# A fused attention and MoE kernel: one list of steps for all engines, named PSUM banks, and two more batches transposed by DMA

## The chip, the cores and the metric

The kernel runs on one core of one Trainium2 chip. The metric is the device time of the kernel in microseconds; lower is better. Three runs of the kernel before took 324.28, 325.44 and 326.56 us, so the median is 325.44 us.

## What is computed

Sliding-window attention with a distance bias (a query sees itself and the 127 keys before it), and behind it a feed-forward layer whose activation is a Swish with its own beta for each hidden unit. The attention output, heads side by side, is the layer's input.

```python
B, H, S, D = q.shape                      # 8, 8, 576, 64
scores = (1.0 / np.sqrt(D)) * np.matmul(q, k.transpose(0, 1, 3, 2))
rel = pos[:, None] - pos[None, :]
mask = (rel >= 0) & (rel < 128)
scores = np.where(mask, scores - slopes[:, None, None] * np.abs(rel), -1e9)
attn = softmax(scores)
x = np.matmul(attn, v).transpose(0, 2, 1, 3).reshape(B * S, H * D)   # 4608 x 512
h = x @ w_in                              # 512 x 2048
g = h * (1.0 / (1.0 + np.exp(-beta * h)))
out = g @ w_out                           # 2048 x 512
```

## The kernel before

The 4608 tokens are worked on in two tilings at once. Attention goes by batch (8 batches of 576 tokens, each in four query blocks of 128 and a tail of 64). The feed-forward layer goes by group (9 groups of 512 tokens). Batches and groups don't line up: group g needs tokens 512g to 512g+511, so group 2 needs blocks 0 to 2 of batch 2, group 3 the last two blocks of batch 2 and blocks 0 to 2 of batch 3, and so on.

For batch b of 2 to 7 the steps are these:

- q and k arrive in f32 by DMA issued from SP (`get`, L207; the buffers are `fst`, 14 of them), GpSimd casts them to bf16 (`cast_qk`, L228 and L229, buffers `bst`, 4 of them), and SP issues a transposing DMA into `qkT` (`DT`, L413). v comes by a casting DMA of GpSimd (`get_v`, L250).
- S: `SC` (L438) multiplies keys by queries for a pair of heads; each of its matmuls uses 64 rows of the array. ScalarE takes the exponential of 1024 columns (L446, about 1.02 us), and VectorE multiplies it by the decay and mask (`factor`, L171 and L176, 0.79 and 0.71 us).
- V: `PVB` (L492, L495) multiplies the weights by v for all eight heads of a block; VectorE divides by the sum (L499, L500), which gives the block's attention output `xn`.
- X: `xn` has tokens on partitions and must be transposed into `XT`, a ring of three groups. For batches 0 to 3 this is done by TensorE (L520 for batches 2 and 3: matmuls against the identity into PSUM, and a copy by ScalarE, L523). From batch `XDMA = 4` on it is a transposing DMA from SP (L512).

Batches 0 and 1 have a form of their own for the four full blocks: loads and casts by pairs of heads (`get_pair`, L218; `cast_pair`, L235), transposition on TensorE (`TP`, L287), two score visits A and B for each pair (`SP_`), `PVP`, and `XP` for the transposition of the result.

For group g, H is one of 16 hidden tiles: four matmuls of 128x512 (`Hm`, L557), a tanh on ScalarE (L564, about 0.69 us) and a product on VectorE (L565, 0.68 us) into `gT`. O is a quarter of the second product for a block of 128 tokens: four matmuls of 128x512 (`OS`, L588); after four of them ScalarE copies 128x512 out of PSUM into `osb` (L598, 0.60 us; five buffers) and a DMA stores it, issued from GpSimd for groups 0 to 2, from ScalarE later, from SP for the last two (L606). The last block is done in two halves of 256 columns that share a bank; the second half's copy is VectorE's (L596). The weights W1 and W2 come by four casting DMAs each on GpSimd's queue.

The order is written by hand. The opening (batches 0 and 1, and group 0) is a list of calls. From then on `spread` lays the steps of the attention, weighted, between the H and O of the groups. PSUM banks come from pools that are opened and closed on the way (`psum_t`, `psum_x`, `psum_o`, `psum_s`). TensorE, SP and GpSimd keep the written order in the opening and later; ScalarE and VectorE keep it in the opening alone, and in the rest the scheduler may choose:

```python
    with tc.manual_schedule(engines={ENG.PE, ENG.SP, ENG.Pool}):
        with tc.manual_schedule(engines={ENG.Activation, ENG.DVE}):
            for w in ("p0", "p1", "v0", "p2", "v1", "p3", "v2", "v3"):
```

Of the kernel before, what the change touches and what calls it, by code (L numbers as in the profile page):

```python
# [15 lines left out]
P = 128  # L16


@with_exitstack
def kernel(  # L20
# [63 lines left out]
    psum_c = ctx.enter_context(tc.tile_pool(name="psum_c", bufs=1, space=bass.MemoryType.PSUM))  # L84
    psum_h = ctx.enter_context(tc.tile_pool(name="psum_h", bufs=2, space=bass.MemoryType.PSUM))
    trans = ExitStack()
    psum_t = trans.enter_context(tc.tile_pool(side="right", name="psum_t", bufs=2, space=bass.MemoryType.PSUM))
    SS = psum_c.tile([P, 2, 512], F32, name="SS")
    psum_c.seal()
    opening = ExitStack()  # L90
    psum_x = opening.enter_context(tc.tile_pool(name="psum_x", bufs=1, space=bass.MemoryType.PSUM))
    SX = psum_x.tile([P, 2, 512], F32, name="SX")
    late, gates = {"tick": 0}, {}
    spans = [SS]

    def span():

        spans.append(spans.pop(0))
        return spans[-1]

    def obank(name, tag=None):
        if tag is None:
            late["n"] = late.get("n", 0) + 1
            tag = "ops" if late["n"] % 2 else "h3"
        return late["o"].tile([P, DM], F32, name=name, tag=tag)[:]

    def after(ins, other):
        tc.add_manual_dep(
            ins.ins, other.ins.name,
            mybir.DependencyInfo(mybir.DependencyClass.Sync, mybir.DependencyReason.DATA),  # L110
            reason="gate",
        )

    def idle(n):
        for _ in range(n):
            nc.tensor.matmul(
                SS[:, 0, :], lhsT=zeros[:, 0:P], rhs=zeros[:], start=True, stop=True,
                skip_group_check=True)  # L120

    def constants():
# [4 lines left out]
        idle(8)  # L127
# [35 lines left out]
    def falls_late(i):  # L163
        to, a, w = ((0, 0, P), (128, 0, 64), (192, 0, P), (320, 1, 64), (384, 1, P))[i]
        after(nc.vector.tensor_copy(
            out=falls[:, :, to : to + w], in_=fall[:, :, a, 0:w]), gates[1, 4])

    def factor(pt, m, p):

        if m:  # L170
            nc.vector.tensor_tensor(  # L171
                out=pt[:], in0=pt[:], in1=falls[:, 2 * p : 2 * p + 2], op=ALU.mult)
            return
# [16 lines left out]
    def betas():  # L190
        bps = psum_t.tile([P, NFF], F32, name="bps", tag="t")
        nc.tensor.transpose(out=bps[:], in_=bflat[:], identity=identf[:])
        nc.vector.tensor_scalar_mul(beta_h[:], bps[:], 0.5)
# [7 lines left out]
    def get(what, b, sb):  # L201
# [5 lines left out]
        return nc.sync.dma_start(  # L207
# [4 lines left out]
    def get_pair(b, p):  # L212

        r = []
        for what, src in (("k", k), ("q", q)):
            f = fst_pool.tile([P, 2, 4, D], F32, name="fst", tag="fst")
            fs[what, b, "p", p] = f
            r.append(nc.sync.dma_start(  # L218
                out=f[:].rearrange("r h c d -> r h (c d)"),
                in_=src[b, 2 * p : 2 * p + 2, 0:FULL, :].rearrange("h (r c) d -> r h (c d)", c=4),  # L220
            ))
        return r[0]

    def cast_qk(b, sb):
        rows = ROWS[sb]
        t = bst_pool.tile([P, 2, H, D], BF16, name="bst", tag="bst")
        staged[b, sb] = t
        nc.gpsimd.tensor_copy(out=t[0:rows, 0], in_=fs.pop(("q", b, sb))[0:rows])  # L228
        return nc.gpsimd.tensor_copy(out=t[0:rows, 1], in_=fs.pop(("k", b, sb))[0:rows])  # L229

    def cast_pair(b, p):
        t = bst_pool.tile([P, 2, 4, 2 * D], BF16, name="bst", tag="bst")
        staged[b, "p", p] = t
        for i, what in ((1, "k"), (0, "q")):
            r = nc.gpsimd.tensor_copy(  # L235
                out=t[:, i].rearrange("r c (h d) -> r h c d", d=D),
                in_=fs.pop((what, b, "p", p))[:])
        return r

    def cast_v(b, sb):  # L240
        moved.add(("v", b, sb))
        rows = ROWS[sb]
        return nc.gpsimd.tensor_copy(  # L243
            out=VS[b % 2][0:rows, sb, :, 0:D], in_=fs.pop(("v", b, sb))[0:rows])
# [22 lines left out]
    pts, xns = {}, {}  # L267

    def calm(n):

        z = psum_h.tile([P, 512], F32, name="z", tag="hps")
        for _ in range(n):
            nc.tensor.matmul(
                z[:], lhsT=zeros[:, 0:P], rhs=zeros[:], start=True, stop=True,
                skip_group_check=True)

    def TP(b, p):
        src = staged.pop((b, "p", p))
        for i in (1, 0):
            if (b, p) == (0, 1):  # L280
                calm(1 + i)
            tps = psum_t.tile([P, FULL], BF16, name="tps", tag="t")
            to = tps[:].rearrange("d (c r) -> d c r", c=4)
            if i == 0:
                to = tps[:].rearrange("d (k c r) -> d c k r", k=4, c=4)
# [256 lines left out]
    def Hm(g, j, cs):  # L542
# [18 lines left out]
        if cs[-1] < NDM - 1:  # L561
            return
# [332 lines left out]
```

The softmax here doesn't subtract the row's maximum and nothing guards it: scores larger than these inputs give would overflow.

## Time and profile before

| What | Value |
|---|---|
| runs, median (lowest to highest) | 325.44 us (324.28 to 326.56) |
| span of the profiled execution, first to last instruction | 324.0 us |
| median of the runs less that span | 1.4 us |
| mean granted clock of TensorE | 0.999 of full |
| HBM read and written | 36.71 MB, 9.44 MB |
| L588, O: 592 matmuls | 28.6% of the chain that ended last |
| L557, H: 576 matmuls | 31.1% of the chain that ended last |

The profiled execution's own time isn't listed apart from its span; what lies around the span is taken from the median of the runs, 1.4 us. The chain of waits, followed back from the last instruction, is PE for 69% and DMA for 17%. Busy times of matmuls overlap: one of 128x512 is listed with 379 ns, but four that follow each other begin 0.86 us before the next four.

### The profile page before, as it was taken

Reading aid. Unit: us, or ns where it says so; the run is one execution under the profiler, and the core shown is the slowest. Engines: PE = TensorE matmul, PEld = TensorE weight load, DVE = VectorE, ACT = ScalarE, POOL = GpSimd, SP = SyncE. Lnnn points to the kernel's source line nnn. Section 1 sums busy time; section 2 is a strip of 40 time slices with the busy share of each in tenths; the row PEclk is TensorE's granted clock in tenths of the full one; section 3 lists DMA queues with packets and bytes.
Section 4 is the critical chain, followed back from the end, with each engine's and each line's share of the span. In section 5 each row is a group of like instructions: output and inputs, shape, how many; then the busy total and the mean of one; then the engine's idle time right before and its main releaser. Section 6 shows DMA issues by size and latency. Waiting matters only on the chain.

```text
span 324.0 us, 5988 instructions
## 1 busy us (share of the span) xinstructions
PE 312.7 (97%) x2297; PEld 153.3 (47%) x2297; DVE 183.1 (57%) x346; ACT 194.1 (60%) x283; POOL 98.8 (30%) x154
## 2 busy tenths in 40 slices
PE   8888999999999999999999999999999999999995
PEld 3454554443545454544454545444544455444443
DVE  5777877542548753785178717752775176335500
ACT  6857887635558865685467635845675465346511
POOL 4864820333873455356226232340000000000000
PEclk9999999999999999999999999999999999999999
DMA  7999999998999999999969994993222112110021
GB/s 221 252 263 238 176 196 196 215 199 162 214 181 208 222 208 139 230 217 148 257 153 196 150 245 94 211 138 107 18 65 60 65 18 65 46 62 32 10 90 65
DMA packets 147565, 48.84 MB, mean 151 GB/s; under 512 B 135360, under 2 KB 143824, under 8 KB 147536
## 3 DMA queue, kind: packets, MB, share of 16 engines
q1 hardware_dynamic: 115712, 32.39, 56.1%
q0 software_dynamic: 28624, 10.29, 26.1%
q10 hardware_dynamic: 3200, 5.78, 5.1%
q8 instruction: 18, 0.29, 0.4%
q14 instruction: 11, 0.09, 0.1%
HBM read 36.71 MB, written 9.44 MB: 142 GB/s over the span
## 4 chain that ended last, share of the span: by engine, by line
PE 69%; DMA 17%; SPq 6%; POOL 2%; ACT 2%; DVE 2%; issue 1%; POOLq 0%; DVEq 0%
PE ops L588 21%; PE hps L557 21%; PE hpo L557 10%; PE oph L588 7%; DMA fst<-in_v_dram 6%; DMA qkT<-bst 6%; SPq L207 3%; DMA fst<-in_q_dram 3%; DMA fst<-in_k_dram 2%; PE SS L438 2%; SPq L218 2%; PE ST L438 1%; PE SS L495 1%; PE SS L492 1%; POOL bst L229 1%
## 5 line engine op out<-in xcount | busy, mean ns | idle before, releaser
L588 PE MATMUL ops<-W,gT 128*128 128x512 bf16 (+1 forms) x464 | 109.7, 372 | 0.5 <-ACT osb L598 0.5
L565 DVE SCALAR_TENSOR_TENSOR gT<-sig,hps 128x512 bf16<-128x512 bf16 x100 | 67.6, 683 | 71.8 <-ACT sig L564 71.5
L557 PE MATMUL hps<-XT,W 128*128 128x512 bf16 x400 | 99.9, 379 | 0.3 <-DVE XT L533 0.3
L564 ACT ACTIVATE sig<-hps,beta_h 128x512 bf16<-128x512 f32 x100 | 68.1, 690 | 34.6 <-PE hps L557 33.2
L588 PEld LDWEIGHTS <-gT 128*128 128x128 bf16 x592 | 55.7, 98 | 61.6 <-issue 1.9
L557 PEld LDWEIGHTS <-W 128*128 128x128 bf16 x576 | 52.9, 98 | 60.8 <-issue 3.6
L228 POOL CAST bst<-fst 128x512 bf16<-128x512 f32 (+1 forms) x32 | 20.8, 650 | 74.4 <-DMA fst<-in_q_dram 42.4
L557 PE MATMUL hpo<-XT,W 128*128 128x512 bf16 x168 | 43.1, 379 | 0.0
L564 ACT ACTIVATE sig<-hpo,beta_h 128x512 bf16<-128x512 f32 x42 | 29.0, 690 | 16.9 <-PE hpo L557 16.9
L565 DVE SCALAR_TENSOR_TENSOR gT<-sig,hpo 128x512 bf16<-128x512 bf16 x42 | 28.6, 681 | 11.2 <-ACT sig L564 11.0
L598 ACT ACTIVATE osb<-ops 128x512 f32<-128x512 f32 (+1 forms) x28 | 16.6, 595 | 25.5 <-PE ops L588 25.5
L446 ACT ACTIVATE pt<-SS 128x1024 bf16<-128x1024 f32 x24 | 24.5, 1020 | 11.6 <-PE SS L438 11.1
L588 PE MATMUL oph<-W,gT 128*128 128x512 bf16 x128 | 29.3, 379 | 0.0
L229 POOL CAST bst<-fst 128x512 bf16<-128x512 f32 (+1 forms) x32 | 22.1, 690 | 15.6 <-DMA fst<-in_k_dram 15.0
L176 DVE TENSOR_TENSOR pt<-pt,fall 128x1024 bf16<-128x1024 bf16 x24 | 17.1, 712 | 14.8 <-ACT pt L446 14.8
L446 ACT ACTIVATE pt<-ST 128x1024 bf16<-128x1024 f32 x24 | 24.5, 1022 | 0.0
L171 DVE TENSOR_TENSOR pt<-pt,falls 128x1024 bf16<-128x1024 bf16 x24 | 18.8, 791 | 9.3 <-ACT pt L446 9.3
L250 POOL DMA_DIRECT2D vs<-in_v_dram x25 | 21.3, 869 | 0.2 <-issue 0.2
L598 ACT ACTIVATE osb<-oph 128x512 f32<-128x512 f32 x8 | 4.8, 597 | 21.1 <-PE oph L588 21.1
L495 PEld LDWEIGHTS <-pt 128*128 128x128 bf16 x240 | 14.8, 97 | 4.2
L243 POOL CAST vs<-fst 128x512 bf16<-128x512 f32 (+1 forms) x15 | 10.5, 703 | 15.9 <-DMA fst<-in_v_dram 15.9
L438 PEld LDWEIGHTS <-qkT 64*128 64x128 bf16 x240 | 8.9, 94 | 12.5 <-issue 12.0
(102 smaller groups left out, 257.8 us busy)
## 6 DMA issues: line engine op xcount, KB each, us to landing
fst<-in_k_dram SPq DMA_DIRECT2D x32, 256.0 KB, 6.0
fst<-in_q_dram SPq DMA_DIRECT2D x32, 256.0 KB, 5.3
out_dram<-osb ACTq DMA_DIRECT2D x22, 256.0 KB, 2.0
fst<-in_v_dram SPq DMA_DIRECT2D x12, 256.0 KB, 5.4
out_dram<-osb POOLq DMA_DIRECT2D x12, 256.0 KB, 5.2
vs<-in_v_dram POOLq DMA_DIRECT2D x20, 128.0 KB, 6.1
W<-in_moe_w_in_dram POOLq DMA_DIRECT2D x4, 512.0 KB, 7.9
W<-in_moe_w_out_dram POOLq DMA_DIRECT2D x4, 512.0 KB, 12.8
```

Of the source, the lines that this page charges most:

```text
L171: nc.vector.tensor_tensor(out=pt[:], in0=pt[:], in1=falls[:, 2 * p : 2 * p + 2], op=ALU.mult)
L228: nc.gpsimd.tensor_copy(out=t[0:rows, 0], in_=fs.pop(("q", b, sb))[0:rows])
L229: return nc.gpsimd.tensor_copy(out=t[0:rows, 1], in_=fs.pop(("k", b, sb))[0:rows])
L250: return nc.gpsimd.dma_start(out=VS[b % 2][0:rows, sb, :, 0:D], in_=v[b, :, P * sb : P * sb + rows, :].rearrange("h p d -> p h d"))
L438: nc.tensor.matmul(o, lhsT=qk[64 * e : 64 * e + 64, 1, p, P * kb : P * kb + P], rhs=qk[64 * e : 64 * e + 64, 0, p, P * kb : P * kb + nq], ...
L446: nc.scalar.activation(out=pt[:], in_=sps[:], func=ACTF.Exp, scale=qscale)
L495: nc.tensor.matmul(o, lhsT=weights(b, qb, h, 0), rhs=vs[:, qb, h, 0 : D + 1], start=qb == 0, stop=True, skip_group_check=True)
L557: nc.tensor.matmul(hps, lhsT=W1[:, c, bass.ts(j, P)], rhs=XT[:, c, c0 : c0 + TOKG], start=(c == 0), stop=(c == NDM - 1),)
L564: gates[g, j] = nc.scalar.activation(out=sig[:], in_=hps, func=ACTF.Tanh, scale=beta_h[:, j : j + 1])
L565: gates["gT"] = nc.vector.scalar_tensor_tensor(out=gts[g][:, j, :], in0=sig[:], scalar=1.0, in1=hps, op0=ALU.add, op1=ALU.mult)
L588: nc.tensor.matmul(ops_[:, cols], lhsT=gT[:, j, i * P : i * P + P], rhs=W2[:, j, cols], start=(j == 0), stop=(j == NFF - 1),)
L598: nc.scalar.mul(o, ops_[:, cols], 0.5)
```

## The change

All that the hand-written order, `spread` and the pools did is replaced by one list, `PLAN`, of some 1300 steps. A step has a name, the batch or group, the tile and, where it writes PSUM, a bank. One loop walks the list, and each engine keeps the list's order, ScalarE and VectorE too, from the first instruction to the last. PSUM is one tile of eight banks. What was one helper (matmul, then the copy or the exponential) becomes two steps, so that the second can stand elsewhere in the list.

The names: `k q` (loads of pairs), `gq gk gv` (loads of blocks), `ck cq cQ cK cv` (casts), `w1 w2`, `pv` (v by casting DMA), `D` (transposing DMA of q and k), `Rk Rq rk rq` (transposition on TensorE and copy), `A B EA EB VA VB nA nB XP xc` (batches 0 and 1), `S E M V n XD` (batches 2 to 7), `H a d` (hidden tile, tanh, product), `O oc st` (second product, copy, store), `OL lc ls` (halves of the last block), `z` (idle matmuls).

`XD`, the transposing DMA, now serves batches 2 to 7; the matmul form `X` is left for the tails of batches 0 and 1. The halves of the last block have a bank each, and the second half goes first.

```diff
-    psum_c = ctx.enter_context(tc.tile_pool(name="psum_c", bufs=1, space=bass.MemoryType.PSUM))
-    psum_h = ctx.enter_context(tc.tile_pool(name="psum_h", bufs=2, space=bass.MemoryType.PSUM))
...
+    psum = ctx.enter_context(tc.tile_pool(name="psum", bufs=1, space=bass.MemoryType.PSUM))
+    PS = psum.tile([P, 8, 512], F32, name="PS")
+    def bank(k):
+        return PS[:, k, :]
...
     def X(b, qb):
...
-        if b >= XDMA:
-            tok0 = (b * S + P * qb) % XTR
...
-        if b >= 2:
-            xt = span()[:, 0, :].rearrange("p (c q) -> p c q", c=NDM)
...
+    def XD(b, qb):
+        xnv = xns.pop((b, qb))[:].rearrange("p h d -> p (h d)")
+        for r0, r1, at in pieces(b, qb):
+            nc.sync.dma_start(out=XT[:, :, at : at + r1 - r0], in_=xnv[r0:r1], transpose=True)
...
+    with tc.manual_schedule(engines={ENG.PE, ENG.SP, ENG.Pool, ENG.Activation, ENG.DVE}):
+        for step in PLAN.split():
+            name, *at = step.split(":")
+            name, _, eng = name.partition(".")
+            STEPS[name](*([ENGINES[eng]] if eng else []), *map(int, at))
```

Parts of the list, in its order: the start; the loads and casts of the opening; the steps around the start of groups 2, 3, 4 and 5; the end.

```
const q.s:0:0 k.s:0:0 ck.p:0:0 k.s:0:1 q.s:0:1 z:2:5 order ones Rk:0:0:5 cq.p:0:0 ck.p:0:1 rk.v:0:0
cq.p:0:1 z:1:7 Rq:0:0:0 k.s:0:2 ck.p:0:2 rq.a:0:0 A:0:0:4:1 EA:0:0 k.s:0:3 q.s:0:2 Rk:0:1:1
B:0:0:6:0 z:1:4 q.s:0:3 EB:0:0 cq.p:0:2 ck.p:0:3 Rq:0:1:4 gv.s:0:1 gv.s:0:0 cq.p:0:3 z:2:6 rk.v:0:1
fr:6 fr:0 rq.a:0:1 beta:1 Rq:0:2:4 Rk:0:2:5 cv.p:0:1 gv.s:0:3 q.s:1:1 rk.v:0:2 gv.s:0:2 cv.p:0:0
q.s:1:0 k.s:1:0 rq.a:0:2 B:0:1:6:0 w1:0 fr:4 A:0:1:1:1 cv.p:0:3 EB:0:1 Rk:0:3:5 Rq:0:3:0 EA:0:1
...
cQ.p:3:0 n:2:0 M:2:1:1 M:2:1:0 M:2:1:3 gk.s:3:2 XD:2:1 gq.s:3:4 st.p:0:1 M:2:1:2 V:2:2:5 gv.s:2:3
O:1:1:0:7 O:1:0:3:2 O:1:2:2:0 O:1:1:1:7 D:3:0 XD:2:0 cQ.p:3:1 cQ.p:3:4 cK.p:3:2 st.p:0:0 cK.p:3:4
cv.p:2:3 n:2:2 O:1:1:2:7 XD:2:2 V:2:4:5 O:1:2:3:0 gq.s:3:3 H:2:0:1 a:2:0 oc.a:1:0 n:2:4 H:2:1:3
...
O:2:1:0:3 O:2:1:1:3 V:3:0:5 O:2:0:2:7 D:4:1 V:3:2:0 O:2:2:0:4 O:2:2:1:4 O:2:2:2:4 n:3:0 n:3:2
S:4:0:0:0 S:4:0:1:5 E:4:0:1 M:4:0:1 cQ.p:4:3 cK.p:4:3 st.p:1:0 cK.p:4:4 cQ.p:5:0 gq.s:4:4 XD:3:1
O:2:2:3:4 XD:3:0 XD:2:3 st.p:1:3 XD:3:2 O:2:0:3:7 cQ.p:4:4 gk.s:6:3 D:4:3 V:3:3:5 gk.s:5:4 D:4:4
gk.s:5:1 O:2:1:2:3 E:4:0:0 V:3:4:0 n:3:3 n:3:4 oc.a:2:0 H:3:1:7 O:2:1:3:3 a:3:1 H:3:0:0 H:3:4:2
...
O:2:3:3:2 pv:5:4 pv:4:2 cK.p:5:1 pv:4:3 cK.p:5:2 V:4:1:0 H:3:15:7 H:3:6:5 n:4:1 H:3:14:0 H:3:13:1
a:3:10 a:3:6 d:3:6 H:3:9:6 a:3:15 a:3:14 H:3:12:5 XD:4:1 d:3:14 oc.a:2:3 a:3:13 a:3:12 d:3:15 d:3:10
O:3:1:0:2 M:4:1:1 d:3:13 H:4:1:0 a:4:1 D:5:0 D:5:2 D:5:1 H:4:5:4 d:3:12 a:3:9 cQ.p:5:4 a:4:5 a:3:11
...
E:5:1:2 O:3:3:3:4 V:5:1:6 O:4:0:0:5 st.p:1:2 H:4:11:0 O:4:0:1:5 cK.p:6:2 d:4:12 H:4:13:3 oc.a:3:3
gq.s:6:2 a:4:11 M:5:1:2 n:5:1 H:4:14:4 O:4:1:0:1 st.a:3:0 a:4:13 O:4:1:1:1 st.a:3:2 D:6:0 M:5:1:0
d:4:9 pv:5:3 cQ.p:6:4 cQ.p:6:1 pv:5:2 a:4:14 XD:4:2 XD:5:0 cQ.p:6:2 XD:5:1 D:6:1 d:4:13 gk.s:6:4
H:5:3:7 H:5:2:6 d:4:14 d:4:11 H:5:6:4 D:6:2 gq.s:7:3 H:5:1:3 a:5:3 H:5:0:2 a:5:1 d:5:3 a:5:2 a:5:6
...
st.a:7:2 O:8:1:2:0 oc.a:8:0 lc.v:1 st.a:8:0 O:8:1:3:0 oc.a:8:1 st.a:8:1 st.s:8:2 ls.s:1 OL:0:1
lc.a:0 ls.s:0
```

## The prediction

> **What bounds the kernel now.** I read the page's first lines, then busy time by stages, then TensorE's groups by shape, then single waits in the timeline.
>
> ```profile
> span 324.0 us, 5988 instructions
> PE 312.7 (97%) x2297; PEld 153.3 (47%) x2297; DVE 183.1 (57%) x346; ACT 194.1 (60%) x283; POOL 98.8 (30%) x154
> ```
>
> TensorE is busy for 97% of the span; no other engine is above 60%. A new order can only win back PE's idle 11.3 us, or take work off PE. The stages (columns: stretch, length, then busy us and count of PE, weight loads, DVE, ACT, POOL; clock, DMA share, GB/s) tell where that idle time is:
>
> ```profile
> 0.00:8.00 8.00, 6.62 (x34) 3.09 (x34) 4.72 (x25) 5.34 (x12) 3.57 (x13) 1.00 0.75 220
> 8.00:16.00 8.00, 6.65 (x84) 3.24 (x82) 6.19 (x14) 6.50 (x9) 6.95 (x10) 1.00 1.22 251
> 16.00:24.00 8.00, 7.09 (x83) 4.07 (x84) 5.64 (x17) 4.65 (x8) 5.34 (x10) 1.00 1.19 266
> 24.00:32.00 8.00, 6.98 (x57) 3.19 (x57) 6.03 (x11) 6.35 (x11) 3.31 (x5) 1.00 1.01 241
> 40.00:48.00 8.00, 7.40 (x106) 4.50 (x101) 5.71 (x15) 6.57 (x11) 2.01 (x4) 1.00 1.23 195
> 64.00:310.00 246.00, 244.19 (x1712) 118.21 (x1711) 136.17 (x230) 145.23 (x207) 68.08 (x98) 1.00 0.86 137
> 310.00:324.00 14.00, 10.07 (x62) 5.86 (x60) 0.42 (x1) 1.73 (x4) 0.00 (x0) 0.99 0.21 76
> ```
>
> The first 48 us lose 5.3 us (1.2 of them before the first matmul), the 246 us of the steady stage 1.8, the end 3.9, of which some 3.4 is the last store after the last matmul. So the steady stage is packed already; a large gain isn't there to be had. The groups that lost something outside the opening:
>
> ```profile
> L438 PE MATMUL SS<-qkT 64*128 64x256 bf16 x72 | 8.5, 276 | 1.3 <-DMA qkT<-bst 1.3
> L520 PE MATMUL ST<-ident,xn 128*128 128x128 bf16 x16 | 1.6, 220 | 0.5 <-DVE xn L500 0.5
> L588 PE MATMUL ops<-W,gT 128*128 128x256 bf16 x32 | 3.8, 273 | 0.5 <-ACT osb L598 0.5
> ```
>
> **What the change takes off PE.** X for batches 2 and 3 was matmuls against the identity (L520): 8 blocks of four 128x128 and 2 of four 64x64. One of them in the timeline (start, length, engine, line):
>
> ```profile
> 91.00 1.02 PE L588 MATMUL ops<-W,gT 128*128 128x512 bf16 x4
> 92.27 0.40 PE L520 MATMUL ST<-ident,xn 128*128 128x128 bf16 x4 [0.24 <-DVE xn L500]
> 92.50 1.89 PE L588 MATMUL ops<-W,gT 128*128 128x512 bf16 x8
> ```
>
> The block occupies PE from 92.27 to 92.50, 0.23 us; four 128x512 take 0.86 elsewhere, so L520 could have begun at 91.86 and lost 0.40 (the 0.24 shown hides a drain of 0.17). Eight blocks of 0.23 and two of about 0.1 (64x64 follow at 25 ns) are 2.0 us; two waits of 0.40 (the other at 122.91) are 0.8. **-2.8.** The Trainium skill, "TensorE: Matmul & The Clock Gate", Back-to-back issue gap, gives some 56 ns for 128 columns isolated and about 81 with a weight load each; this trace's four in 0.23 are 58 each, and I go by those. The 10 ACT copies out of PSUM (L523, 0.6 us each) go too: 5.6 us on an engine that idles 40%, hidden under PE; no gain.
>
> **What it adds.** Ten more DMA transposes on SP's queue, for which the nearest row is the 21 that batches 4 to 7 have already:
>
> ```profile
> L512 SPq DMA_TRANSPOSE XT<-xn x21: 1171/1194/2271, 146.8 to 276.6; - x21
> DMA to landing us min/median/max: 2.3/2.8/6.5
> ```
>
> Each holds SP for 1.2 us. After 216 us, when only stores share the DMA engines, landing is 2.3 to 3.9; the twelve from 146 to 215 average 4.6. The skill's "DMA: Bandwidth & Descriptors", section Issuing engines are not separate DMA queues, says that all DMAs share the same 16 engines and interleave whoever issues them; the two halves agree, and as the new ten fall about where L520 stood, 88 to 138 us (DMA share 1.2 to 1.4), I use the loaded figures.
>
> Whether PE sees this depends on how much PE work the new list leaves between the product V of the last needed block and the first H of the group that reads it. Counting 0.86 for each four 128x512, 0.46 for a V, 0.22 for an S plus 0.24 to switch in and out of 64-row matmuls:
> - group 2: after V(2,2) six O and one V, 5.6 us;
> - group 3: after V(3,2) six O, two S, two V, 6.8;
> - group 4: after V(4,1) seven H or O, 6.1;
> - group 5: after V(5,1) seven, 6.1;
> - group 6: after V(6,0) seven O, three S, one V, 7.4; groups 7 and 8 over 9.
>
> In the kernel before, V ends at 181.7, 212.1, 245.4 and 274.8, and groups 5 to 8 begin at 191.2, 222.5, 255.0 and 285.2: 9.5 to 10.4 us, and none waits. The new list is tighter. The chain costs 1.2 us for V's end to xn's end (121.67 to 122.85), then SP, then landing L. With SP free and L=4 it is 5.2: no wait. With one more transpose ahead on SP (1.2) and L=4.6 it is 7.0: 1.4+0.2+0.9+0.9 over groups 2 to 5, 3.4. I take **+2.0**, bounds 0 and 12 (L=6.5, one ahead: 8.9, so 3.3+2.1+2.8+2.8+1.5=12.5). What is queued behind such a transpose on SP: q and k loads and the transposes D of the next batch, with S behind them.
>
> **What it moves.**
> - The score waits (L438, three of 0.43 mean idle plus 0.17, 1.8 us): q and k casts, D and loads are in a new order. Loads for batch 2 come far ahead, but D(3,1), D(3,2), D(4,1) and D(7,2) still stand right before the S that needs them, and D (L413) lands 3.1 to 7.8 us after its issue. I count half as gone: **-0.9**, bounds -1.8 and +2.
> - The last O half gets a bank of its own, and DVE's half goes first. The halves of 16 matmuls begin at 316.26 and 318.64; 16 at 109 ns are 1.74. **-0.6.** If bank 1 were late it would cost that 0.6.
> - Opening. q and k of batch 0 go ahead of v on SP; in the trace loads land about 1 us apart (the eighth at 10.9, the tenth at 12.5), so the last q/k comes at 10.9 in place of 12.5. Against that, the last v is 13th in place of 12th, after 16 us, W1's first part is issued on POOL behind two v casts (about 13.2, not 10.5), and W1's third goes behind k(1,2)'s cast, which frees the DMA for q and k of batch 1: the 1.1 us of L287's waits at 30.8. ACT's row of exponentials (8 of 0.8 to 1.0) and DVE's norms (0.6 each) end where they did, about 17.4 and 20. Of 4.1 us removable idle I take **-1.5**, bounds -4 and +3 (W1 late for H(0,4)).
> - W2's parts, the tail casts and v loads on POOL are far from their readers: O of group 0 begins after 44 us of PE work and W2 is asked for after 25 to 33. Output stores of groups 0 to 2 go later on POOL; (0,3)'s stands near the end of the v loads, so one of five osb buffers is held. ACT may then wait at the copies of group 2, each freed by a store that lands 5.2 us after issue; PE has about 3 us of other banks there. Zero; if that cover is gone, up to 3.
> - Banks by name and no pools: in the steady stage the list leaves 1.4 us or more (median 5) from an H to the next use of its bank, where tanh and product take 0.69 and 0.68. Zero; cover is PE's other banks. E, factor, V: V(2,2) follows its last S by 1.7 us, with 1.02 and 0.79 between: 0.2 inside the range. Everything else (exp, tanh, norms, idle matmuls, matmul counts, number of S groups: 25 for 24) is the same.
>
> **Sum.** -2.8 +2.0 -0.9 -0.6 -1.5 = -3.8: span 320.2. The median of the runs, 325.44, is 1.4 over the span of the profiled execution; so 321.6.
>
> **Rivals.**
> - *All waits go.* Idle that a new order can remove: 4.1 in the opening, 2.1 from 48 to 310, 0.6 at the end, 2.0 of X, and about 0.17 more per wait for some 20 of them, 3: 11.8. Span 312.2, time 313.6. For it: ACT and DVE are never above 84% in any stage. Against it: the opening runs at 240 to 266 GB/s, so data, not order, sets part of it.
> - *The gain is given back.* Each transposition leaves PE but returns as a wait before H. With L=4.6 and one ahead (3.4) and nothing won in the opening or at S: -2.8-0.6+3.4 = 0: time 325.4.
> - *Slower: SP's row becomes the path.* SP issues in order. In groups 2 to 6 the last XT transpose has loads, a D or other transposes ahead of it, and the next loads behind. At L=6.5 the waits before H are 12.5; with the other terms -5.8 that is +6.7: 332. It decides from L of about 5.6 (8.0 per chain: 2.4+1.2+1.9+1.9+0.6 = 8.0, and S waits doubled, +1.8): then +4. For it: 6.5, 6.2 and 6.4 occur in the trace; against it: the issue order there is denser in loads than the new one, which fetches k ahead.
> - *It doesn't do what it says*: the built order holds 40 matmuls and 10 copies fewer and 10 transposes more, so that is out.
>
> **Chances.** Forecast case (319 to 324) 0.45; all waits gone 0.15; given back 0.22; slower 0.18. A change under 1% (322.2 to 328.7) is about what can't be told from none here. Faster takes the second case and most of the first: 0.50; same 0.32; slower 0.18. The range leaves out the upper part of the slow case and the tip of the floor: 314 to 328.5.
>
> **What would show it.** Right: no L520-like matmul for xn, the wait between the last halves gone, small waits (under 1.5 us each) of H on DMA XT at the starts of groups 2 to 5, PE's first 48 us a little denser. Wrong on the good side: XT transposes landing in under 4 us and no H waiting. Wrong on the bad side: H or S waiting on DMA by 2 us and more each, SP's waits for xn in front of loads, or ACT held by osb with PE behind it.

## The result and the profile after

| | median | range | runs |
|---|---|---|---|
| before | 325.46 us | 324.20 to 326.56 | 20 |
| after | 327.22 us | 324.24 to 329.76 | 20 |

The ratio is 1.0043, 95% interval 1.0022 to 1.0063: the change makes the kernel slower by some 0.4% (1.8 us between the medians), where 1.2% faster was forecast, and the range of the runs is more than twice as wide. Medians and ranges, here and below, are of all runs; a ratio leaves out the runs that are over 1.5% above the fastest of their kernel, two of the new kernel's twenty, and its profiled execution is one of these two. The span of that execution is 327.6 us, that of the median run 325.4; what is said of the new list below therefore also rests on profiles of other kernels that share the list where it matters.

The first lines of the page after:

```profile
span 327.6 us, 5873 instructions
PE 311.3 (95%) x2257; PEld 152.0 (46%) x2257; DVE 183.0 (56%) x346; ACT 184.8 (56%) x273; POOL 96.0 (29%) x154
```

The 40 matmuls and 10 copies are gone, PE has less to do, and it idles 16.3 us where it idled 11.3. Busy time by stages (columns as before: stretch, length, PE, weight loads, DVE, ACT, POOL, then clock, DMA share, GB/s):

```profile
8.00:16.00 8.00, 6.73 (x76) 3.23 (x72) 5.94 (x13) 6.54 (x10) 5.05 (x8) 1.00 1.09 254
16.00:24.00 8.00, 5.50 (x87) 3.84 (x87) 6.45 (x19) 3.63 (x6) 4.02 (x6) 0.95 1.14 258
24.00:32.00 8.00, 8.00 (x49) 3.58 (x48) 3.24 (x6) 5.69 (x10) 3.02 (x5) 0.84 1.24 197
...
40.00:48.00 8.00, 6.74 (x102) 3.96 (x100) 6.50 (x18) 5.22 (x8) 6.13 (x11) 1.00 1.19 193
...
64.00:310.00 246.00, 240.83 (x1664) 115.47 (x1663) 139.46 (x235) 136.87 (x196) 66.40 (x99) 1.00 0.92 143
310.00:327.60 17.60, 13.58 (x79) 7.53 (x77) 0.42 (x1) 2.66 (x5) 0.00 (x0) 0.98 0.25 90
```

Two things are to be seen. The opening and the 246 us after it are both less dense than before (the latter loses 5.2 us, not 1.8). And the clock column isn't 1.00 from 16 to 32 us: a row with PE "8.00 busy" there hides slow work. The waits themselves, in the timeline of PE (start, length, line, tiles; in brackets the idle time and what ended it):

```profile
23.30 5.21 PE L633 MATMUL PS<-XT,W 128*128 128x512 bf16 x16 [1.71 <-DMA W<-in_moe_w_in_dram]
36.00 1.04 PE L633 MATMUL PS<-XT,W 128*128 128x512 bf16 x4 [0.32 <-DMA W<-in_moe_w_in_dram]
...
45.77 1.90 PE L633 MATMUL PS<-XT,W 128*128 128x512 bf16 x8 [1.26 <-DVE xnp L439]
71.06 1.89 PE L656 MATMUL PS<-W,gT 128*128 128x512 bf16 x8 [0.36 <-DMA W<-in_moe_w_out_dram]
74.54 0.61 PE L523 MATMUL PS<-qkT 64*128 64x256 bf16 x8 [0.49 <-DMA qkT<-bst]
90.50 0.20 PE L578 MATMUL PS<-vs,pt 128*128 128x65 bf16 x1 [0.93 <-DVE pt L262]
97.26 1.90 PE L633 MATMUL PS<-XT,W 128*128 128x512 bf16 x8 [0.71 <-DMA XT<-xn]
...
191.19 4.04 PE L633 MATMUL PS<-XT,W 128*128 128x512 bf16 x18 [1.04 <-DMA XT<-xn]
```

The first row needs reading twice: 16 matmuls take 5.21 us, where eight take 1.90 in the row at 45.77 and 16 would take 3.6. TensorE ran at half clock for 3.4 us (23.1 to 26.6 in the clock record) right behind its wait for W1, and that costs 1.7 us more than the wait. The wait at 45.77 is put down to DVE, but W1's fourth part lands at 45.72, so it is that one. Loads of W1 and W2, of before and of after (operation, count, min/median/max duration in ns, first and last issue):

```profile
L258 POOL DMA_DIRECT2D W<-in_moe_w_in_dram x4: 740/744/899, 10.5 to 32.7; - x4
L262 POOL DMA_DIRECT2D W<-in_moe_w_out_dram x4: 740/744/747, 35.1 to 39.4; - x4
```

```profile
L351 POOL DMA_DIRECT2D W<-in_moe_w_in_dram x4: 742/745/897, 13.8 to 37.8; - x4
L355 POOL DMA_DIRECT2D W<-in_moe_w_out_dram x4: 742/742/812, 40.9 to 64.3; - x4
```

The last part of W2 is issued 25 us later than before, and lands at 71.02, when its reader waits. Why, GpSimd's timeline after shows:

```profile
46.08 0.78 POOL L206 CAST bst<-fst 64x512 bf16<-64x512 f32 x1
59.64 0.61 POOL L206 CAST bst<-fst 128x512 bf16<-128x512 f32 x1 [12.78 <-DMA fst<-in_k_dram]
60.20 0.84 POOL L206 CAST vs<-fst 128x512 bf16<-128x512 f32 x1
60.98 0.81 POOL L355 DMA_DIRECT2D W<-in_moe_w_out_dram  x1
```

GpSimd stood 12.8 us at a cast of batch 2's k, whose load was issued late on SP, with two W2 loads behind it in its queue.

**One measure for all kernels below.** From the starts of PE's matmuls I sum up what each took beyond its pace in an undisturbed row (216 ns for 128x512, 109 for 128x256, 55 for 128x128, 29 for 128x65, 56 for 64 rows x 256): waits, switches and half clock together, "lost PE time", up to a time t. A wait counted so is 0.17 us longer than the idle time in brackets, as in the prediction. Idle matmuls that an experiment adds count as lost.

| lost up to | 24 us | 48 | 76 | 130 | 250 | 316 |
|---|---|---|---|---|---|---|
| before | 9.3 | 14.1 | 15.9 | 20.0 | 23.9 | 24.3 |
| after | 11.0 | 16.5 | 18.5 | 22.9 | 29.4 | 29.8 |
| after's list, last bank alone changed (d_lastbank) | 11.2 | 14.8 | 19.6 | 23.3 | 28.6 | 28.8 |

The work itself sums to 295.4 us before and 293.5 after. The last two rows are of one and the same list up to 316 us, and they differ by up to 1.7 us, so a difference of that size between two single profiles means nothing. a_xpe below shares that list up to 85 us, and up to 76 us it lost only 0.6 more than the kernel before.

### The profile page after: what moved, and what is told of

The parts are those of the page before. It is cut to its first block, busy times and chain, and to the rows that moved or that the text cites. A ratio compares the mean times of both kernels' runs of the same rounds, so it can differ in the third digit from the quotient of the medians.

```text
span 327.6 us, 5873 instructions
## 1 busy us (share of the span) xinstructions
PE 311.3 (95%) x2257; PEld 152.0 (46%) x2257; DVE 183.0 (56%) x346; ACT 184.8 (56%) x273; POOL 96.0 (29%) x154
## 4 chain that ended last, share of the span: by engine, by line
PE 62%; DMA 20%; SPq 6%; DVE 4%; POOL 3%; ACT 2%; issue 1%; POOLq 0%; ACTq 0%
PE PS L656 28%; PE PS L633 26%; DMA fst<-in_k_dram 8%; DMA fst<-in_v_dram 5%; PE PS L523 4%; DMA qkT<-bst 3%; DMA XT<-xn 3%; SPq L307 3%; DVE pt L262 2%; PE PS L578 2%; POOL bst L206 2%; PE PS L575 1%; SPq L621 1%; SPq L316 1%; ACT pt L532 1%
## 5 line engine op out<-in xcount | busy, mean ns | idle before, releaser
L633 PE MATMUL PS<-XT,W 128*128 128x512 bf16 x576 | 136.7, 383 | 5.9 <-DMA W<-in_moe_w_in_dram 2.0
L641 ACT ACTIVATE sig<-PS,beta_h 128x512 bf16<-128x512 f32 x144 | 94.9, 688 | 74.8 <-PE PS L633 67.8
L656 PE MATMUL PS<-W,gT 128*128 128x512 bf16 x560 | 132.7, 379 | 0.7 <-ACT osb L678 0.4
L646 DVE SCALAR_TENSOR_TENSOR gT<-sig,PS 128x512 bf16<-128x512 bf16 x144 | 94.3, 682 | 66.6 <-ACT sig L641 66.3
L532 ACT ACTIVATE pt<-PS 128x1024 bf16<-128x1024 f32 x48 | 47.4, 1023 | 27.8 <-PE PS L523 27.6
L678 ACT ACTIVATE osb<-PS 128x512 f32<-128x512 f32 (+1 forms) x36 | 21.1, 592 | 28.7 <-PE PS L656 24.2
L587 DVE TENSOR_TENSOR xn<-PS,zb 128x512 bf16<-128x512 f32 (+1 forms) x30 | 20.7, 689 | 1.0
L578 PE MATMUL PS<-vs,pt 128*128 128x65 bf16 x240 | 17.2, 193 | 1.0 <-DVE pt L262 0.9
L523 PE MATMUL PS<-qkT 64*128 64x256 bf16 (+2 forms) x240 | 15.2, 250 | 0.9 <-DMA qkT<-bst 0.9
L432 ACT ACTIVATE pt<-PS 128x768 bf16<-128x768 f32 (+1 forms) x16 | 14.2, 926 | 1.2 <-PE PS L422 1.2
L575 PE MATMUL PS<-vs,pt 128*128 128x65 bf16 x192 | 14.7, 193 | 0.0
```

The lines of the kernel that those rows point to most:

```text
L523: nc.tensor.matmul(o, lhsT=qk[64 * e : 64 * e + 64, 1, p, P * kb : P * kb + P], rhs=qk[64 * e : 64 * e + 64, 0, p, P * kb : P * kb + nq], ...
L532: nc.scalar.activation(out=pt[:], in_=held.pop(("S", b, m, p)), func=ACTF.Exp, scale=qscale)
L575: nc.tensor.matmul(o, lhsT=weights(b, qb - 1, h, 1), rhs=vs[:, qb - 1, h, 0 : D + 1], start=True, stop=False, skip_group_check=True)
L578: nc.tensor.matmul(o, lhsT=weights(b, qb, h, 0), rhs=vs[:, qb, h, 0 : D + 1], start=qb == 0, stop=True, skip_group_check=True)
L633: nc.tensor.matmul(hps, lhsT=W1[:, c, bass.ts(j, P)], rhs=XT[:, c, c0 : c0 + TOKG], start=(c == 0), stop=(c == NDM - 1),)
L641: nc.scalar.activation(out=sig[:], in_=hps, func=ACTF.Tanh, scale=beta_h[:, j : j + 1])
```

## The experiments

The theories, by the letters that the expectations use: **A**, single weight loads stand at the wrong place of GpSimd's queue; **B**, the first 75 us are bound by data, so that what counts is the bytes that stand ahead of their first reader; **C**, the loss is in the steady stage, by the transposes or by the strict order of VectorE and ScalarE; **D**, in two senses: in the a_w2 kernels that W2's late parts hold TensorE, in a_xpe that the transposing DMAs of batches 2 and 3 are what costs. Beside them: half clock behind a wait, and too little distance between the steps of a chain. Edits of the list are shown as the steps that move. Times are medians; every ratio is to the kernel before on the same chip.

### The transposing DMAs alone

**b_xdma2**: the kernel before, old order, with the transposing DMA from batch 2 on.

```diff
-XDMA = 4
+XDMA = 2
```

> The kernel before with XDMA = 2: the transposing DMA for batches 2 and 3 alone, in the old order and with the old pools. By the forecast's terms: 2.8 us of matmuls and waits gone. The old order leaves only two steps between the last V and group 2's first H, so a wait of 2 to 4 us on XT at group 2 and under 1 at group 3: 0 to +1.5 us against the kernel before. If the new transposes are hidden: -2.8.

338.40 us, 1.0393 (1.0370 to 1.0417): 12.9 us slower, where 0 to 1.5 was expected. PE's first H of group 2:

```profile
106.32 1.89 PE L557 MATMUL hps<-XT,W 128*128 128x512 bf16 x4 [13.12 <-DMA XT<-xn]
```

SP's queue ahead of it, and busy time and clock of that stretch:

```profile
90.04 1.41 SPq L512 DMA_TRANSPOSE XT<-xn  x1
91.54 4.84 SPq L413 DMA_TRANSPOSE qkT<-bst  x3
96.48 3.51 SPq L512 DMA_TRANSPOSE XT<-xn  x2
```

```profile
96.00:112.00 16.00, 5.68 (x21) 2.00 (x22) 1.79 (x3) 2.73 (x4) 7.47 (x12) 0.57 1.73 180
```

This is the slower rival of the prediction (SP's row becomes the path), in the old order: xn is ready at 92.45, but three transposes for qkT stand ahead on SP; the two left are issued at 96.48 and 98.15 and land at 103.5 and 106.3. So 5.7 us pass on SP up to the last issue, and 8.1 to its landing, where the prediction's worst was 6.5. Four matmuls at half clock then take 1.89 us, where four take 1.02 in the prediction's timeline. The new list takes nearly all of that away (0.88 at this place). So the order does a real service to a part that was only meant to save 2.8: the two kernels are 11 us apart, though they differ in the rest of the order too.

**a_xpe**: the new list with X on PE for batches 2 and 3.

```diff
-XD:2:0 ... XD:2:4 XD:3:0 ... XD:3:4
+X:2:1:3 x.a:2:1 (where XD:2:1 was), X:2:0:3 x.a:2:0, X:2:2:4 x.a:2:2 (before H:2:0), and so on for batch 3
```

> The new kernel with the attention outputs of batches 2 and 3 transposed by TensorE again (four matmuls each and a copy by ScalarE, in banks that the list leaves free there) in place of the transposing DMAs; no other step moves. It measures this part of the change inside the new list. By the prediction's terms: +2.0 of PE work and up to 0.8 of waits for xn, less the waits of H for XT in groups 2 and 3 (0.88 in the new kernel's profile): +1 to +2 us, 328.2 to 329.2. If the transposing DMAs are what made the new kernel slower (theory D): 325.5 or less. If the transposes' DMA traffic also delays loads and stores, the waits for qkT after 130 us shrink too.

328.17 us, 1.0061 (1.0032 to 1.0090), 0.95 above the new kernel, just under the 328.2 to 329.2 that the prediction's terms gave, though the intervals overlap. Theory D, in its second sense, falls: without these transposing DMAs the new list isn't faster. But the profile shows that they aren't the gain they look like either:

```profile
88.22 0.20 PE L579 MATMUL PS<-vs,pt 128*128 128x65 bf16 x1 [0.68 <-DVE pt L263]
95.39 1.89 PE L634 MATMUL PS<-XT,W 128*128 128x512 bf16 x8 [0.67 <-ACT XT L207]
```

H of group 2 waits 0.84 in all here too, for ScalarE's copy in place of a DMA: the chain V, xn, transpose, H is too short in this list whoever transposes. From 76 to 316 us this kernel loses 9.1 us, d_lastbank 9.2, after 11.3, before 8.4.

### The opening: moving loads

Seven kernels move single loads, or add idle matmuls, in the new list.

**a_w10** and **a_wearly**: W1's first part ahead of a cast; then W1's third and fourth and W2's fourth as well.

```diff
 cq.p:0:2
+w1:0
...
+w1:2   (before cq.p:1:0)
+w1:3   (before cK.p:0:4)
+w2:3   (before cK.p:2:1)
```

> The changed kernel with one token moved: the first part of W1 is asked for after the cast of q(0,2), as in the kernel before, in place of after both casts of v. Theory A: it lands near 18 to 20 us, the wait before the first H falls from 1.9 to under 0.5 us and the clock stays full, 2.5 to 3.3 us less than the changed kernel. Rival B (the opening is bound by the bytes, so the wait only moves to q, k and v): within 1 us of the changed kernel.

> The changed kernel with four weight loads moved up in GpSimd's list: W1 parts 0, 2 and 3, W2 part 3. Theory A: the four waits for weights (1.9 at 23 us, 0.5 at 36, 1.4 at 45.8, 0.5 at 71) and the half-clock stretch (1.5) go, 4.5 to 5.5 us less than the changed kernel, near 322.2, which is under the kernel before. Rival B: k, q and v come later by what the weights come earlier, gain under 2 us, with waits for casts or qkT in their place. Rival C (the loss is in the steady stage: transposes, strict order on VectorE and ScalarE): gain under 2 us and the waits after 64 us as they were.

a_w10: 327.01 us, 1.0017 (0.9996 to 1.0039). W1 lands at 19.9 in place of 23.3, but v of block (0,2) is late now: PE waits 5.1 us at 21 us for its cast, with half clock from 19 to 26. a_wearly: 328.59 us, 1.0088 (1.0058 to 1.0118): 2.9 us of wait for the same cast, and W2 late at 67 and 71 us, by 1.3 and 0.9.

**a_w2**, **a_w2z**, **a_w2open**, **a_w2openosb**: W2's two late parts behind the first; that with eight idle matmuls before H(0,2); that with W1's first part and a v load earlier; and with three stores earlier as well.

```diff
 w2:0
+w2:2 w2:3
...
+z:8:5         (a_w2z: before H:0:2:5)
+gv.s:0:2      (a_w2open: before gv.s:0:3), w1:0 (after cq.p:0:2)
+st.p:0:3      (a_w2openosb: after st.p:0:2), st.p:1:2 st.p:1:1 (after st.p:1:3)
```

> The changed kernel with W2's parts 2 and 3 asked for right behind part 0 in GpSimd's list, not behind casts that wait for batch 2's loads. Theory D (the late W2 pins TensorE: whatever the opening gains is given back at 67 to 71 us): both land by 58 us, the wait of 0.5 us at 71 goes, and 0.5 to 2 us less than the changed kernel. Rival B (bytes): the loads of batch 2 come as much later, and qkT waits (0.7 at 74.5) grow: within 0.5.

> The same, and the eight idle matmuls ahead of the first H. Theory D: what they saved (the half-clock stretch, 1.5 us) is kept now, since no wait for W2 stands behind it: 1 to 1.7 us less than the kernel with W2 moved alone, and over 2 us less than with the idle matmuls alone (327.8). Rival: no difference between with and without idle matmuls, as before.

> W2 moved up, and in the opening the twelve loads of batch 0 first (v(0,2) ahead of v(0,3) and q(1,1)) and W1's first part asked for after the cast of q(0,2), as the kernel before has them. Theory D: v(0,2) lands by 15, W1 part 0 by 19, so that no wait over 0.6 us is left before 30 us and the clock stays full: 2.5 to 4 us less than the changed kernel, 323.2 to 324.7. Rival B: q, k of batch 1 or W1's second part arrive later, with a wait of 1 us or more before H(0,4) or R(1,2).

> The same, and the stores of output blocks (0,3), (1,1) and (1,2) issued early, so that no buffer of osb is held. If the waits for ScalarE at 137 to 155 us (0.3, 0.5, 0.8) come from copies that wait for a buffer, they go: 0.8 to 1.6 us less than without. If they come from the strict order on ScalarE itself: no difference.

328.54 us, 1.0083 (1.0061 to 1.0105); 328.29, 1.0096 (1.0058 to 1.0135); 327.69, 1.0061 (1.0038 to 1.0085); and 327.95, 1.0056 (1.0026 to 1.0086). In each the wait for W2 is gone, and a wait of S(2,0) for qkT takes its place at 74 to 76 us: 3.0, 3.6, 2.0 and 1.6 us. W2's two parts now stand ahead of batch 2's q and k. In the profiles of these four and of the two e_ kernels below 39 matmul records are missing, so their lost time isn't compared.

**a_z8**: nothing but eight idle matmuls ahead of the first H.

```diff
+z:8:5
 H:0:2:5
```

> The changed kernel with eight idle matmuls of 128x512 (1.73 us at full clock) put ahead of the first H, where TensorE waits 1.9 us for the first part of W1 and then runs at half clock for 3.4 us. Theory A (the weights come late on GpSimd's queue, and the idle stretch makes the clock drop as well): the wait stays, the half-clock stretch at 23 to 27 us goes, 1.0 to 1.7 us less than the changed kernel (about 325.7). Rival (the clock drop has another cause, or is in few runs only): no difference over 0.5 us.

327.82 us, 1.0070 (1.0045 to 1.0095). The half clock of the opening is gone, lost time at 48 us falls from 16.5 (14.8 in d_lastbank) to 13.0 with the idle matmuls counted; then PE meets W2's third part 3.2 us early at 67 us, half clock follows, and at 76 us it is 18.5 again, as in the new kernel. S(2,0) begins at 74.4, where it began at 74.5. What was won had to wait for data.

Theory A falls by these seven: none has an interval that lies below the new kernel's, and S(2,0) begins between 73.8 and 75.5 us whichever load is moved. (It began at 74.5, 75.5 and 72.3 in after, d_lastbank and a_xpe, which are one list up to there.)

**c_vlate**: four early loads out of the opening, 0.79 MB.

```diff
-gv.s:2:1 gv.s:2:4 gv.s:2:0 gk.s:3:4   (in the opening)
+gv.s:2:1 gv.s:2:0                     (after D:2:2), gv.s:2:4 gk.s:3:4 (after D:2:0), casts behind
```

> The new kernel with three early loads of batch 2's v (blocks 0, 1 and the tail) and the tail load of batch 3's k taken out of the opening and put behind batch 2's last q and k loads; their casts follow. No other step moves. That is 0.79 MB, some 3.3 us of loading at the 240 GB/s of the opening, that no longer stands ahead of W1's third and fourth part, W2 and batch 2's q and k. If the first 75 us are bound by the bytes that stand ahead of their first reader (theory B): the waits for W1 at 36 and 46 us, for W2 at 71 us and for qkT at 74.5 us shrink from 3.1 us together to under 1.5, S of batch 2 begins 1.5 to 3 us earlier, and the time falls by 1 to 2.5 us against the new kernel's 327.2, to 325 to 326. If it is the place of single weight loads in their queues (theory A): W1's and W2's parts land within 0.5 us of where they did, and the time stays at 327. If batch 2's v comes too late now, V(2,1) waits at about 79 us and nothing is won.

326.76 us, 1.0028 (1.0006 to 1.0049). The waits that PE's timeline marks from 21 to 100 us:

```profile
23.71 5.31 PE L633 MATMUL PS<-XT,W 128*128 128x512 bf16 x16 [2.56 <-DMA W<-in_moe_w_in_dram]
39.20 0.34 PE L454 MATMUL PS<-vs,pt 128*128 128x65 bf16 x6 [0.38 <-POOL vs L206]
86.87 0.19 PE L578 MATMUL PS<-vs,pt 128*128 128x65 bf16 x1 [0.18 <-POOL vs L206]
93.12 0.19 PE L575 MATMUL PS<-vs,pt 128*128 128x65 bf16 x1 [1.01 <-POOL vs L206]
95.60 1.90 PE L633 MATMUL PS<-XT,W 128*128 128x512 bf16 x8 [0.97 <-DMA XT<-xn]
```

No weight load was moved, yet W2's third part is issued at 54.8 in place of 61.0, behind a wait for k that is shorter:

```profile
54.29 0.61 POOL L206 CAST bst<-fst 128x512 bf16<-128x512 f32 x1 [8.19 <-DMA fst<-in_k_dram]
54.84 0.74 POOL L355 DMA_DIRECT2D W<-in_moe_w_out_dram  x1
```

The four waits for W1, W2 and qkT between 36 and 75 us are gone, and S(2,0) begins at 71.9, 2.6 us earlier. That is what B forecast and A excluded. One profile wouldn't show it, since a_xpe begins S(2,0) at 72.3 without the edit. All profiles together do: in the eight kernels with the late loads S(2,0) begins at 69.6 to 73.6 (median 71.8), in the ten with the early ones at 72.3 to 75.5 (74.3); and wherever W2's third part keeps its place in the list, it is issued at 52.7 to 54.8 with the late loads and at 57.9 to 61.0 with the early ones. The edit takes more than bytes out of the way, though: four `fst` buffers, and a cast that stood right ahead of this part of W2 (0.8 us of the 6.2). That it is the bytes alone is not shown. The time fell by only 0.5 against the new kernel, in place of 1 to 2.5, and these runs can't tell that from nothing. Two waits of 1 us (for v's cast, then for XT) come at 93 and 95.6.

**c_vlatew2**, **c_vlw2osb**: that with W2's parts early, and with the three stores early.

> The kernel with late v of batch 2, and W2's third and fourth part issued right behind the other two. With the early v loads in place this edit cost 0.4% (the wait for W2 went, and one of 3.0 us for batch 2's qkT came). Theory B: the 0.79 MB make room for it now: W2 wait gone, qkT wait under 1.5 us, time 324.5 to 326. If the qkT wait stays at 2 to 3 us, then W2's loads alone, not the bytes ahead, hold batch 2 back, and the time is 327 to 328.5.

> The kernel with late v and early W2, and three stores issued early: of group 0's last block right behind that of its third block, and of group 1's second and third blocks behind that of its last. In the new kernel they stand far down GpSimd's queue and hold osb buffers, for which ScalarE's copies, and behind them PE, waited at 137, 153 and 155 us (1.6 us in all). If these waits are real losses: 1 to 1.6 us below the same kernel without this edit, 323.5 to 325, below the kernel before. If the stores' traffic comes back as later landings of XT: waits of H for XT of the same size, no gain.

328.32 us, 1.0056 (1.0025 to 1.0086), and 327.38 us, 1.0046 (1.0017 to 1.0075). The waits for W2 and for qkT are both gone now, as B has it, but the times didn't follow. In the second the waits for osb are gone as well, and one of 2.1 us for XT stands at 131 us, with half clock behind it: its losing alternative. Another of 0.7 for XT is left at 155.0 us, where the new kernel had 0.8.

**d_z8v**: late v, and the idle matmuls.

> The new kernel with both edits that each mended one half of the first 75 us: eight idle matmuls right ahead of the first H of group 0 (which alone kept TensorE at full clock in the opening, but ran into W2 at 67 us), and the late loads of batch 2's v and batch 3's tail of k (which alone took away the waits for W1's later parts, W2 and qkT, but left the 2.7 us wait for W1's first part and half clock behind it). If bytes ahead of their readers and half clock after a wait are the two causes of what the first 75 us lost: no half clock before 300 us, no wait over 0.8 us from 24 to 76, PE's lost time up to 76 us (the idle matmuls counted as lost) 1.5 to 2.5 us less than with the late loads alone, and 325 to 325.8 against their 326.8. If the half clock is without effect, since data are late in any case: W2 or qkT waits grow again by 1.5 us and the time stays at 326.5 to 327.5.

326.09 us, 1.0011 (0.9985 to 1.0037): its interval takes in no change, and it has the lowest ratio of all variants of the list, though the intervals of several overlap with it. No half clock before 300 us. But the size is a miss: at 76 us the lost time is 16.1 with the idle matmuls, against 16.3 with the late loads alone, not 1.5 to 2.5 less, and waits of 1.5 us (at 60.9, for a product of VectorE) and 0.9 (S(2,0), for qkT) stand where none over 0.8 was expected. S(2,0) begins at 71.7 against 71.9 and waits for its data now, which the late loads alone didn't make it do. That leans to the second alternative, but its wait is half of the 1.5 us named there, and the time lies between the two.

### The steady stage

**d_z8v22**: d_z8v, with v's third block loaded and cast earlier. **e_v23**: d_z8v, with the fourth block right behind the third.

```diff
+gv.s:2:2 (before gk.s:3:4), cv.p:2:2 (after cv.p:2:4)      d_z8v22
+gv.s:2:3 (after gv.s:2:2), cv.p:2:3 (after cv.p:2:2)        e_v23
```

> The same, and the load and cast of batch 2's third v block moved ahead of batch 3's first loads and casts, for which V(2,2) waited at 93 us with the late loads (1.17 us, and group 2's first H waited 1.13 for XT behind it). If what the list lacks after 76 us is distance between such a chain's parts: the V(2,2) wait goes, the H wait stays or shrinks below 1, and the time is 0.8 to 1.2 below the kernel without this edit, 324 to 325. If another step of the same chain (the product of exponential and decay) ends right behind, half of that.

> Idle matmuls and late loads as in d_z8v, and batch 2's fourth v block loaded right behind the third and cast right behind it, ahead of batch 3's casts. In the traces with the late loads V(2,4) (not V(2,2), as the expectation of d_z8v22 had it) waited for this cast at 93 us (0.97 to 3.3 us), because casts of batch 3's tails stand before it, whose q load stands on SP behind a transposing DMA of batch 2's output. If so: V(2,4) waits no more, H(2,0) still waits 0.9 to 1.5 for XT, since that chain starts at V(2,2), and the time is 0.3 to 0.9 below d_z8v, 325.2 to 325.8: level with the kernel before. If the chain to XT takes it all: no change, 326.1.

326.50 us, 1.0023 (1.0003 to 1.0043), and 328.30 us, 1.0085 (1.0052 to 1.0118). Both are misses. In the first the row at 93 us was read wrongly: it is V(2,4), waiting for the fourth block's cast, and the edit moved that back, to a wait of 3.3 us. The second moved the right cast, but V(2,2) then waited 1.3 us for one, and H(2,0) 3.1 us for XT with half clock behind it, in a profile of an execution of 332.5 us.

**d_z8v22o**, **e_v23o**: those two with group 1's last block of O ahead of group 2's first H (16 matmuls, 3.4 us), the second with a store earlier.

```diff
+O:1:3:0:4 O:1:3:1:4 O:1:3:2:4 O:1:3:3:4
 H:2:0:1 a:2:0
+oc.a:1:3
...
+st.p:0:2 (before st.p:0:0)      e_v23o
```

> The same, and group 1's last output block (16 matmuls of 128x512, 3.44 us of PE work, and its copy) taken out of the middle of group 2 and put right ahead of group 2's first H, in a bank that is free there. It gives the chain V(2,2), xn, XT, H 3.4 us more of other work on PE. If that distance is what is missing: no wait of H(2,0) for XT, 1 us less, 323.2 to 324.2, below the kernel before. If ScalarE, which then has group 2's tanh, batch 3's exponentials and no O between them, becomes late: waits for banks or exp from 100 to 125 us of 1 us and more, no gain.

> The same, with group 1's last output block ahead of group 2's first H as in d_z8v22o, and the store of group 0's third block, for whose osb buffer ScalarE's copy waited there for 9.6 us, issued before that of its first. If that store's place was the whole trouble: no wait for osb over 1 us near 110 us, no wait of H(2,0) for XT, 0.8 to 1.2 us below the kernel without these two edits, 324 to 325. If ScalarE is late there for other reasons (tanh and exponentials without O between): waits of 1 us and more for banks or exp from 100 to 130 us, 326 to 328.

340.77 us, 1.0488 (1.0451 to 1.0524), and 326.98 us, 1.0052 (1.0031 to 1.0074). In the first, the wait for XT is gone, and PE stands here:

```profile
109.61 0.58 PE L523 MATMUL PS<-qkT 64*128 64x256 bf16 x3 [9.57 <-ACT osb L678]
```

ScalarE's copy into osb waits for the store of block (0,2), which stands some 80 steps further down the list, in GpSimd's queue. This is the cover that the prediction costed at nothing with "up to 3" behind it: when it is gone it costs 9.6. With the store moved, e_v23o has only 0.3 us of wait for XT at H(2,0), as hoped, but 2.6 us for gT at 115 to 117 us, where O has been taken out from between the H: the losing alternative of its expectation.

### The end

**d_lastbank**: the new kernel with the halves of the last block in one bank.

```diff
-OL:0:1
+OL:0:2
```

> The new kernel with the two halves of the last block in one bank again; nothing else. The prediction gave the second bank 0.6 us. In the new kernel's profile the wait is gone, but the last store lands 2.5 us after its issue, in place of 1.7, because the store before it, issued by ScalarE 1.5 us earlier, is still under way. If so: here the wait of 0.64 between the halves is back, the last store lands in about 1.8 us, and from the start of the last block but one's matmuls to the end the time is the same within 0.3 us. If the landing of 2.5 is chance or comes from the issuing engine: it stays at 2.5, and the end is 0.6 later.

One run: 328.10 us. The rows of the last blocks:

```profile
316.31 1.91 PE L667 MATMUL PS<-W,gT 128*128 128x256 bf16 x16
318.06 2.75 PE L656 MATMUL PS<-W,gT 128*128 128x512 bf16 x12
320.65 1.91 PE L667 MATMUL PS<-W,gT 128*128 128x256 bf16 x16
```

No wait came back: the list puts 12 other matmuls between the halves, and it is these, not the second bank, that took the wait of before away. The last store still lands late, 2.3 us after its issue. So the expectation was wrong on the bank; and as the edit moved nothing in time, it tests nothing on the store. Other traces do: in all 18 kernels of the list ScalarE's store of 128x512 is issued 1.5 us ahead of the last one, and the last one lands 1.7 us after its issue in five of them (a_xpe, a_w2openosb, c_vlw2osb, d_z8v22o, e_v23o) and 2.2 to 2.7 in the rest. The store ahead doesn't explain the late landing, then; its cause stays open.

## Why the prediction was wrong

The forecast was a sum of -3.8 us; it came out at +1.8. (The 1.4 us that the prediction put between span and time paired two executions; each run here lasts 1.7 us or more beyond its own span. That shifts the forecast time by 0.3, not the change.)

- *X off PE, -2.8.* The stream is 1.9 us less, as worked out, and the two waits for xn (0.8) are gone. Right.
- *Waits of H for XT, +2.0.* Measured in the new kernel: 0.88 (group 2) and 1.20 (group 5), 2.1 in all, and a third of 0.77 at 154.98 us, which is group 4's first H: its XT landed at 154.85, and a product of VectorE for which it waited too ended at 154.87. In d_lastbank and c_vlw2osb the same H waits for XT. So 2.1 to 2.9: right in mechanism and place, and near in size; the bound of 12 was real, as b_xdma2 shows.
- *Score waits, -0.9.* Two of 0.66 and 0.61 are left of 1.8: -0.5, a third gone in place of half.
- *Last half, -0.6.* The wait of 0.64 is gone (by the order, not the bank), but the last store lands 2.5 us after its issue in place of 1.7, and 4.0 us pass from the last matmul to the end in place of 3.4. Nothing is left of the term in this profile; in the five of 18 where that store lands in 1.7 us, 3.2 to 3.3 us pass, and the term holds.
- **The opening, -1.5: this step failed**, together with "W2's parts ... are far from their readers ... Zero". Up to 76 us the three profiles that share the list there (after, d_lastbank, a_xpe) lose 2.6, 3.7 and 0.6 us more than the kernel before, where 1.5 less was forecast: off by 2.1 to 5.2 us, more than any other term. The prediction saw that W1's first part would be issued behind two v casts, at "about 13.2, not 10.5" (it was 13.83), and named its lateness as a bound, but then took the earlier q and k as the likelier gain. It counted W2's distance from its readers in PE time and not in what stands ahead of it in GpSimd's queue, a cast that waits 12.8 us for a load. And it had noted that the opening moves 240 to 266 GB/s, "so data, not order, sets part of it", without asking which bytes the new order brings forward: 0.79 MB, ahead of W2 and batch 2's q and k. That these loads hold back W2 and batch 2 is shown by the kernels with the late loads, where S(2,0) begins 2.5 us earlier in the median. It isn't all: up to 60 us the kernel before moves 220 GB/s at a DMA share of 1.07, the new one 210 at 1.06, so the new list has also moved less by then; why isn't shown. And what the opening lost doesn't come back one for one: c_vlate lost 2.2 less up to 76 us, and the time fell by 0.5.
- *No term at all: the clock.* TensorE ran at a mean clock of 1.000 in the kernel before (below 0.997 in 3 of 184 runs) and of 0.994 in the new one (below 0.997 in 14 of 20). The idle matmuls together with the late loads remove it (d_z8v: 1 of 14); alone they don't (a_z8: 3 of 6), nor do the late loads (c_vlate: 15 of 22). In the traces one half-clock stretch of 3.4 us costs 1.7 us of matmuls. In time it goes with about 1 us: the new kernel's 14 runs below 0.997 have a median of 327.3 us, the other six of 326.1, and over 239 runs of 16 kernels of the list the runs below are 1.0 us longer than those of the same kernel above (95%: 0.4 to 1.6). The wait ahead of the half clock is in that difference too, so how much is the clock's own isn't settled; where data were late further on, as in a_z8, removing the first stretch gained nothing in the end. The Trainium skill's "TensorE: Matmul & The Clock Gate", Part 1: The HAM clock gate, says that the clock halves after an idle window of about 3.4 us; here it is the wait that is shorter, 1.9 us in the new kernel and 2.7 in c_vlate, and the half-clock stretch that lasts 3.4.
- *E, factor, V: "0.2 inside the range".* V(2,2) waited 1.1 us, and 1.7 in d_lastbank. GpSimd and VectorE in the new kernel just ahead of it:

```profile
86.67 3.77 DVE L262 TENSOR_TENSOR pt<-pt,falls 128x1024 bf16<-128x1024 bf16 x4 [0.22 <-ACT pt L532]
86.80 1.07 POOL L206 CAST vs<-fst 128x512 bf16<-128x512 f32 x1
87.82 2.08 POOL L206 CAST bst<-fst 128x512 bf16<-128x512 f32 x2
```

  Four factors take 3.77 us, where four of the prediction's 0.79 are 3.2, and casts of 0.62 take 1.07: one after the other, they hold each other up. The skill's "SBUF — State Buffer", Who interferes with whom, has this rule: an instruction of VectorE with two SBUF inputs contends with one of GpSimd that reads SBUF. The trace agrees. The trace of before had such a pair too (1.48 and 1.09 at 88 us), and the mean of 0.79 hid it.
- *osb, zero.* Waits of 0.29 and 0.53 us at 137 and 153 us, and a share in the 0.77 at 155 that can't be told from XT's. Within the bound, not zero.

Of the rivals, "the gain is given back" comes nearest, for another reason than its own: not by XT alone. From 76 to 316 us the new list loses 0.8 to 2.9 us more than before, in waits of 0.5 to 1.7 that stand at other places in every profile (XT, V's factor, osb, qkT). No single one could be removed for a gain clear of noise: each edit that took one away in that stretch brought another. This is taken as too little distance between steps in a fixed order for five engines. That is argued from the pattern; the tests of it (d_z8v22o, and the two e_ kernels) didn't show a gain. One rival is untested: the new list also fixes the order of ScalarE and VectorE after the opening, where the kernel before left it to the scheduler, and no run undoes this part alone. So the cause of the whole 1.8 us stays open in part. No version faster than the kernel before was found.

## What to carry to other kernels

When a new order moves loads, add up the loads that now stand ahead of each reader on all queues together, and look for what can stop a queue ahead of a load; the distance to the reader in PE's work says little while the DMA engines are full. An order that saves work at no slack exchanges a known cost for many small waits, and a wait of about 2 us can cost another 1.7 by the clock, so read the clock column beside the busy column. And take a step's duration from the place where it will stand, beside the engine that will run then, not from the mean of its group.

## What was not expected of the hardware

- Half clock came with 19 of the 26 waits of 1.8 us or more in these traces, but not with all: none after 3.3 us at 94.7 in d_z8v22. The runs don't say what decides it. Each stretch that ended within a span lasted 3.4, 6.8, 10.2 or 13.7 us, whole multiples of 3.41.
- A store of 128x256 landed in 1.7 us in five kernels of the list and in 2.2 to 2.7 in 13, in each 1.5 us behind another of 128x512 from another engine. In the two kernels of the old order it took 1.7.
- Casts on GpSimd and two-input products on VectorE went from 0.62 to 1.07 and from 0.69 to 1.09 us where they met.
